# Split attention and a Fourier gate on one core: the expected flags' program in line with a late guard, sines of one token block rotated into the others, and a new written order

## The chip, the cores and the metric

The kernel runs on one core of a Trainium2 chip. The time is the device time of one execution in microseconds. A core has five engines that this kernel uses: TensorE (PE; its weight loads appear as PEld), VectorE (DVE), ScalarE (ACT), GpSimd (POOL) and SyncE (SP, which here issues most loads and stores). Each engine works through its own instructions strictly in their order and waits on semaphores for the others. The chip's DMA engines move data between HBM and the on-chip memory (SBUF); PSUM is the memory that matmuls write.

## What is computed

The attention takes q, k and v of shape 4 x 8 x 768 x 64. A flag for each of the 8 heads says whether it is a retrieval head (full causal attention) or not (4 sink columns and a window of 64). The inputs given mark heads 0, 2 and 6 as retrieval heads. Its output, 4 x 768 x 512, goes through a gate with a circular convolution over the 768 positions.

```python
scores = scale * np.matmul(q, k.transpose(0, 1, 3, 2))
causal = rel >= 0
stream_keep = causal & (is_sink | in_win)
mask = np.where(retr, full_mask, stream_mask)
scores = np.where(mask, scores, -1000000000.0)
a = np.exp(scores - np.max(scores, axis=-1, keepdims=True))
a = a / (np.sum(a, axis=-1, keepdims=True) + 1e-09)
attn_out = np.matmul(a, v)
...
proj = x @ w_proj
x1, x2, x3 = proj[..., :D], proj[..., D:2 * D], proj[..., 2 * D:]
X2 = np.fft.rfft(x2, n=S, axis=1)
H = np.fft.rfft(filter_fft, n=S, axis=0)[None, :, :]
y = x1 * np.fft.irfft(X2 * H, n=S, axis=1) * x3
return y @ w_out
```

## The kernel before

**Tiling.** The 32 (batch, head) items are worked on as 16 pairs of heads, four to a batch. Pair n belongs to batch n // 4 and to one of four kinds: RL, LL, RR or LL (R a retrieval head, L a local one), so that the blocks of scores that are computed at all are known when the program is built. The 768 tokens are six blocks of 128.

**Steps of a pair.** Loads of k, q and v (lk, lq, lv) on SP's queue; casts to bf16 (ck, cq, cv); six transposes each of k and q on PE (T, line 1447) and their copies out of PSUM (E, a copy of 128 x 768); score chunks on PE (sc, line 1492), to which a bias for masked positions is added by a matmul of the identity with the table btab (sb, line 1505) in the first four pairs, while later pairs mask after the exponential by a product (mk); the exponential on ScalarE (ex, line 1511); the product with v on PE (at, line 1556); the reciprocal of the row sums (rec, line 1562) and the normalised output f_attn (nm, line 1573) on VectorE. The columns kx and v_x are small copies that give the local heads their sink columns. Sums and differences of the two halves of a sequence (fe, fd, both f_fo) start the Fourier transform of the pair (W, line 1617; later pairs use thirds, uv and br).

**Steps of a batch.** Once its four pairs are done, the batch's spectrum X (line 1660), its products with the filter's spectrum HAB (pa, pb, pc on tiles P and m), the inverse transform c (line 1725), the three projections x1, x2, x3 (line 1695), the products that give gy (g, line 1714 and 1718, and y), and the output matmuls o (line 1758) with their evictions oe (f_o) and stores st. The filter's own spectrum F (line 1293) is made once, from the sums and differences of its two halves (fold, line 1285).

**The tables at the start.** The Fourier matrix G, 128 x 6 x 3 x 128 in bf16, is made of sines and cosines on the chip: integer angles (angle) and numbers of turns (turns) for three blocks of token positions, their difference (wrap, line 1201), its absolute value (size, line 1206), and four sine activations over all three blocks (sin1, sin2, cos1, cos2, line 1214). The causal and window masks are the seven 128 x 128 tables of mtab, cut out of ones on GpSimd (mtab1 in the opening; mtab2 and mtab3 at lines 1165 to 1183, behind the first casts); btab (line 1187) is made from mtab on VectorE.

**The two programs.** An opening runs first, which also compares the flags in memory with the expected ones (check). Every engine then loads the result into a register and branches (lines 1862 and 1863): with other flags a general program is run, written out in full in a sequence of its own (ORDER), else the patterned one.

**What sets the order.** The order of the patterned program is written out by hand in the text FAST: each word is an operation, @ names one of four PSUM slots (two banks each) and /v, /s, /p the engine where there is a choice. The opening's order is in OPENING. The operations are issued in that order on their engines, nothing is moved later. BLANKS gives the sizes of three groups of matmuls on a tile of zeros (blank0 to blank2, line 1143), 17 in all. The last block of 128 output rows is done in two halves (oe3.5 and oe3.6), which share one PSUM tile.

## Time and profile before

| what | us |
|---|---|
| three runs | 188.08, 188.29, 188.73 |
| median of the runs | 188.29 |
| span of the profiled execution, first to last instruction | 188.0 |
| TensorE busy | 171.7 |
| VectorE busy | 152.6 |
| ScalarE busy | 143.3 |
| GpSimd busy | 64.1 |

No time beside its span is given for the profiled execution, so the 0.3 us between span and median stand for what lies around it. In the rows below, a number such as L1447 is the line of the kernel. An arrow points from what is read to what is written; f_ is a prefix of the patterned program's tiles. A row of a timeline gives the start and the length of a run of like instructions and, in brackets, the idle time before it and what ended that. Busy times of TensorE are modelled from overlapping matmuls, so a busy TensorE isn't one at its peak.

### The profile page before, as it was taken

To read this page: it belongs to the slowest core of one execution; us is meant where nothing else is said; L and a number is where in the kernel's file an instruction comes from. 1 tells how busy PE (TensorE), PEld (TensorE's weight loads), DVE (VectorE), ACT (ScalarE), POOL (GpSimd) and SP (SyncE) were. 2 spreads that over 40 slices of the span, in tenths; PEclk is the share of its full clock that TensorE was granted. 3 is DMA by queue.
4 is the path that set the end of the run, shared out by engine and by line. 5 is a ranking of instruction groups with operands and counts; after the bars stand their busy time and mean duration, and the time that the engine had idled before them with its cause. 6 is when DMAs were issued, how large, how long until landed. Compare 5 with 4: busy or idle time off the path is not lost.

```text
span 188.0 us, 4376 instructions
## 1 busy us (share of the span) xinstructions
PE 171.7 (91%) x1688; PEld 103.9 (55%) x1704; DVE 152.6 (81%) x301; ACT 143.3 (76%) x191; POOL 64.1 (34%) x96
## 2 busy tenths in 40 slices
PE   0889996989999999999999999999999999999960
PEld 0346773644585556565556656475567644565430
DVE  6559676968999998998799999999799996388720
ACT  6689995879997998987999999899895526613330
POOL 3368750992080094443210111311406405400200
PEclk9999999999999999999999999999999999999998
DMA  5999999699999899999899988688942205300363
GB/s 182 309 271 281 194 187 287 151 260 228 218 210 203 180 192 210 184 232 234 193 249 257 225 180 176 137 138 225 127 125 55 112 2 157 122 3 0 113 248 104
DMA packets 77695, 33.67 MB, mean 179 GB/s; under 512 B 66850, under 2 KB 74082, under 8 KB 77666
## 3 DMA queue, kind: packets, MB, share of 16 engines
q1 hardware_dynamic: 74576, 30.29, 70.4%
q0 software_dynamic: 2944, 2.88, 10.1%
q8 instruction: 15, 0.25, 0.6%
q10 hardware_dynamic: 146, 0.13, 0.2%
q14 instruction: 14, 0.11, 0.2%
HBM read 24.64 MB, written 6.29 MB: 165 GB/s over the span
## 4 chain that ended last, share of the span: by engine, by line
PE 65%; DVE 14%; DMA 7%; POOL 4%; ACT 3%; issue 2%; SPq 0%; POOLq 0%; DVEq 0%
PE f_x_ps L1695 18%; PE f_X_ps L1660 10%; PE f_out_ps L1758 8%; PE f_c_ps L1725 7%; PE f_sc L1492 6%; PE f_att L1556 6%; DMA qk_ahead<-in_q_dram 4%; DMA f_qk_f<-in_q_dram 3%; DVE f_attn L1573 2%; ACT f_pT L1511 2%; PE f_W_ps L1617 2%; DVE f_P L1110 2%; PE f_sc L1505 2%; DVE f_fo L1110 1%; DVE turns L1736 1%
## 5 line engine op out<-in xcount | busy, mean ns | idle before, releaser
L1511 ACT ACTIVATE f_pT<-f_sc 128x1024 bf16<-128x1024 f32 (+3 forms) x68 | 58.7, 918 | 3.7 <-PE f_sc L1492 3.2
L1695 PE MATMUL f_x_ps<-f_xT,f_wproj 128*128 128x384 bf16 x256 | 46.7, 326 | 0.4 <-DVE f_attn L1573 0.3
L1695 PEld LDWEIGHTS <-f_wproj 128*128 128x128 bf16 x256 | 23.9, 98 | 16.5 <-issue 1.6
L1660 PE MATMUL f_X_ps<-f_wproj,f_xh 128*128 128x512 bf16 x92 | 22.3, 379 | 0.2
L1758 PE MATMUL f_out_ps<-f_wout,f_gy 128*128 128x512 bf16 x86 | 21.7, 379 | 0.3
L1492 PE MATMUL f_sc<-f_qkT 64*128 64x128 bf16 (+3 forms) x248 | 20.3, 250 | 0.0
L1725 PE MATMUL f_c_ps<-f_Gi,f_P 128*128 128x384 bf16 x96 | 18.4, 326 | 0.2 <-DVE f_gy L1714 0.2
L1110 POOL TENSOR_TENSOR f_fo<-f_attn 128x384 bf16<-128x384 bf16 x13 | 12.3, 954 | 15.0 <-DVE f_attn L1573 14.8
L1736 DVE TENSOR_TENSOR turns<-angle,f_c_ps 128x384 bf16<-128x384 f32 x32 | 16.3, 548 | 1.3 <-PE f_c_ps L1725 0.8
L1556 PE MATMUL f_att<-f_v_aug,f_pT 128*128 128x65 bf16 x392 | 17.2, 193 | 0.0
L1556 PEld LDWEIGHTS <-f_pT 128*128 128x128 bf16 x472 | 16.0, 97 | 2.1 <-issue 0.4
L1107 ACT COPY f_o<-f_out_ps 128x1024 f32<-128x1024 f32 (+2 forms) x12 | 10.2, 854 | 8.7 <-PE f_out_ps L1758 7.8
L1573 DVE TENSOR_TENSOR f_attn<-f_att,f_rec 128x768 bf16<-128x768 f32 x16 | 15.3, 955 | 0.6
L1492 PEld LDWEIGHTS <-f_qkT 64*128 64x128 bf16 x248 | 10.6, 94 | 9.3 <-issue 7.0
L1660 PEld LDWEIGHTS <-f_xh 128*128 128x128 bf16 x96 | 9.0, 98 | 10.3 <-issue 0.7
L1107 ACT CAST f_xh<-f_W_ps 128x768 bf16<-128x768 f32 x13 | 10.5, 807 | 4.5 <-PE f_W_ps L1617 2.3
L1758 PEld LDWEIGHTS <-f_gy 128*128 128x128 bf16 x92 | 8.6, 98 | 9.3 <-DVE f_gy L1718 0.3
L1107 ACT CAST f_X<-f_X_ps 128x1024 bf16<-128x1024 f32 x10 | 10.2, 1016 | 4.6 <-PE f_X_ps L1660 4.5
L1531 DVE TENSOR_TENSOR f_pT<-f_pT,mtab 128x1024 bf16<-128x1024 bf16 (+1 forms) x18 | 12.1, 688 | 1.4 <-ACT f_pT L1511 1.4
L1447 PE MATMUL f_qkT_ps<-identity,f_qk_bf 128*128 128x128 bf16 x96 | 7.9, 225 | 5.6 <-DVE f_qk_bf L1101 5.2
L1725 PEld LDWEIGHTS <-f_P 128*128 128x128 bf16 x96 | 9.0, 98 | 6.5 <-issue 0.6
L1110 POOL TENSOR_TENSOR f_br<-f_fo,f_uv 128x256 bf16<-128x256 bf16 x6 | 4.6, 765 | 21.3 <-DVE f_uv L1110 12.3
(132 smaller groups left out, 329.9 us busy)
## 6 DMA issues: line engine op xcount, KB each, us to landing
f_v_f<-in_v_dram SPq DMA_DIRECT2D x32, 192.0 KB, 4.4
out_dram<-f_o SPq DMA_DIRECT2D x17, 256.0 KB, 2.3
qk_ahead<-in_k_dram SPq DMA_DIRECT2D x6, 384.0 KB, 6.3
qk_ahead<-in_q_dram SPq DMA_DIRECT2D x6, 384.0 KB, 6.3
qk_ahead<-in_k_dram SPq DMA_DIRECT2D x10, 192.0 KB, 4.3
qk_ahead<-in_q_dram SPq DMA_DIRECT2D x10, 192.0 KB, 4.9
f_wproj<-in_moe_w_proj_dram POOLq DMA_DIRECT2D x6, 256.0 KB, 7.2
out_dram<-f_o SPq DMA_DIRECT2D x3, 512.0 KB, 4.4
```

Source lines behind the costliest of these rows:

```text
L1107: nc.scalar.copy(out=out, in_=in_)
L1110: (nc.gpsimd if now["engine"] == "p" else nc.vector).tensor_tensor(out, a, b, op)
L1492: nc.tensor.matmul(sc[:, bank, col:col + 128 * cnt], lhsT=keys, rhs=qkT(n)[rows, 0, 128 * i:128 * (i + cnt)], start=(col == 0 or not biase ...
L1511: nc.scalar.activation(out=pT(n)[:, c, :, 0:w], in_=held[f"sc.{n}.{c}"][:, :, 0:w], func=AF.Exp, scale=SCALE)
L1531: nc.vector.tensor_mul(some, some, near(c)[:, None].to_broadcast([128, 2, cols, 128]))
L1556: nc.tensor.matmul(att[:, hh, 65 * i:65 * i + 65], lhsT=pT(n)[:, c, bank, col:col + 128], rhs=values, start=(z == 0), stop=(z == len(here) ...
L1573: nc.vector.tensor_mul(attn(n).rearrange("p i hh d -> p hh i d"), rows[:, :, :, 0:64], held[f"rec.{n}"][:, :, :, None].to_broadcast([128, ...
L1660: nc.tensor.matmul(ps[:, u, :], lhsT=xh(b)[:, cc, chain, 128 * part:128 * part + 128], rhs=wproj()[:, cc, DM:2 * DM], start=(cc == 0), sto ...
L1695: nc.tensor.matmul(ps[:, s, 0:HS], lhsT=wproj()[:, cc, part * DM + cb * 128:part * DM + (cb + 1) * 128], rhs=xT(b)[:, cc, s * HS:s * HS + HS],
L1725: nc.tensor.matmul(ps[:, r, 0:HS], lhsT=P(b)[:, t, u, ch], rhs=Gi()[:, tile_no], start=(m == 0), stop=(m == 2))
L1736: fn(conv[:, half * HS:half * HS + HS], held[f"evs.{b}.{cb}"], held[f"c_ps.{b}.{cb}"][:, 1, 0:HS])
L1758: nc.tensor.matmul(ps[:, i % 2, :], lhsT=gy(b)[:, cb, i * 128:(i + 1) * 128], rhs=wout()[:, cb, :], start=(cb == 0), stop=(cb == NC - 1))
```

## The change

The branch at the start is gone. The opening and the patterned program run in line whatever the flags are. The comparison with the expected flags gives a number differ; near the end the guard looks at the reciprocals of all row sums, which now stay in one tile (recs): they have to lie between 2^-100 and 2^100 (gd0 to gd2; gd3 adds up 128 partitions by a 1 x 1 matmul; gd4 joins this with differ). All engines then load that value (flag), and behind the last store an If runs a general program, now made of loops, where it isn't zero. The bias constant of btab becomes 2^100.

The sines are made for one block of 128 positions alone (base, fp32) and rotated into the other two by a third of a turn: two scalings (gr) and four products (gm) on VectorE, one cast (gc) on GpSimd and three small ones (gs). Angles, turns, wrap and size shrink to a third. mtab2 joins the opening on GpSimd. Seven blank matmuls (warm) run in the opening; the 17 others are in eight groups. The two halves of the last output block get PSUM tiles of their own. The sequence FAST is new, and some operations change engines: of the 16 copies E, VectorE makes 10 instead of 4.

```diff
-BLANKS = (8, 3, 6)
+WARM = 7
+BLANKS = (2, 2, 2, 2, 3, 2, 2, 2)
...
-table sin0 tcol par fcol0 fcol1 ident mblank mtab0v quarter tfrac turns0 check angle0 mtab1 parb
+table mblank sin0 tcol par fcol0 fcol1 ident warm mtab0v quarter tfrac turns0 check angle0 mtab1 mtab2 parb
...
-angle1 turns1 angle2 ck1/p cq0/p turns2 lq2 ones0 ck0/v wrap1 T0.1@0 wrap2 blank0@1 wrap0 sin2 size E0.1/s sin1 lk2
+ck0/s mtab3 blank1@0 cq0/v wrap0 sin2 ones0 size T0.1@1 kz2 kz0 T0.0 ck1/p sin1 kz1 btab cq1/p E0.1/v E0.0/v lk3 cos1
...
-        nc.vector.tensor_scalar(out=btab(), in0=mtab(), scalar1=32768.0, scalar2=-32768.0, op0=ALU.mult, op1=ALU.add)
+        nc.vector.tensor_scalar(out=btab(), in0=mtab(), scalar1=FAR, scalar2=-FAR, op0=ALU.mult, op1=ALU.add)
...
-    trig("cos1", 0, 0, 256, lambda: G()[:, 0:4:3])
+    trig("cos1", 0, 0, 256, lambda: base()[:, 0:4:3])
...
+    @op("gc")
+    def _():
+        ev(G()[:, :, 0], base())
+    for i in range(2):
+        scaled(f"gr{i}", lambda i=i: turned()[:, :, i], lambda i=i: base()[:, 1 - i:5 - i:3], KAPPA if i == 0 else -KAPPA)
...
+                nc.vector.scalar_tensor_tensor(
+                    out=G()[:, tiles, m], in0=base()[:, tiles], scalar=0.5 if (u, m) == (0, 1) else -0.5,
+                    in1=turned()[:, u], op0=ALU.mult, op1=ALU.subtract if (u, m) == (1, 2) else ALU.add)
...
+    @op("flag")
+    def _():
+        pre["reg"] = nc.values_load(pre["other"][0:1, 0:1], min_val=0, max_val=1)
...
-    reg = nc.values_load(other[0:1, 0:1], min_val=0, max_val=1)
-    with tc.If(reg != 0, preferred_fallthrough_block=False) as cmp:
-        general(tc, ahead, pre, q, k, v, is_retrieval, n_sink, window, moe_w_proj, moe_filter_fft, moe_w_out, out)
-    with cmp.Else():
-        patterned(tc, ahead, pre, q, k, v, int(n_sink), int(window), moe_w_proj, moe_filter_fft, moe_w_out, out)
+    patterned(tc, ahead, pre, q, k, v, int(n_sink), int(window), moe_w_proj, moe_filter_fft, moe_w_out, out)
+    with tc.If(pre["reg"] != 0, preferred_fallthrough_block=False):
+        general(tc, local, q, k, v, int(n_sink), int(window), moe_w_proj, moe_filter_fft, moe_w_out, out)
```

How the order moves is shown at three places, as the instructions stand on an engine. The first is VectorE from the last part of the opening to the first copies of kT and qT (tfrac and the check's operations stand ahead of these rows); qk_ahead with 65 or 66 holds k and q of pair 0, f_qk_bf_2974 and f_qk_bf_135 their casts. Before:

```order
L1030 TENSOR_SCALAR angle<-fcol,tcol 128x384
L987 TENSOR_SCALAR par<-par 128x1
L1862 TENSOR_LOAD other
L1863 COMPARE_AND_BRANCH
L1196 TENSOR_SCALAR angle<-fcol,tcol 128x384 x2
L1101 CAST f_qk_bf_2974<-qk_ahead_65 128x768
L1201 SCALAR_TENSOR_TENSOR angle<-turns,angle 128x384 x3
L1206 TENSOR_SCALAR f_size<-angle 128x1152
L1101 COPY f_qkT_3005<-f_qkT_ps_2983 128x768
L1101 COPY f_qkT_3046<-f_qkT_ps_3039 128x768
L1187 TENSOR_SCALAR f_btab<-mtab 128x896
```

In the changed program, from the cast on, with tfrac and the check (want to differ):

```order
L546 CAST f_qk_bf_135<-qk_ahead_66 128x768
L417 TENSOR_SCALAR tfrac<-tcol 128x3
L1349 MEMSET want 1x8
L1352 MEMSET want 1x1 x3
L1353 TENSOR_SCALAR zeros<-flags 1x16
L1354 TENSOR_TENSOR local<-zeros 1x8
L1355 TENSOR_TENSOR differs<-local,want 1x8
L1356 TENSOR_REDUCE differ<-differs 1x1
L475 TENSOR_SCALAR angle<-fcol,tcol 128x384
L413 TENSOR_SCALAR par<-par 128x1
L670 SCALAR_TENSOR_TENSOR angle<-turns,angle 128x384
L675 TENSOR_SCALAR f_size<-angle 128x384
```

and directly behind them:

```order
L637 TENSOR_SCALAR f_btab<-mtab 128x896
L546 COPY f_qkT_175<-f_qkT_ps_150 128x768 x2
L682 TENSOR_SCALAR f_turned<-f_base 128x2x128
L546 COPY f_qkT_208<-f_qkT_ps_194 128x768
L682 TENSOR_SCALAR f_turned<-f_base 128x2x128
L546 COPY f_kx_170<-f_qkT_208 128x4x4
```

The cast (now of q0; k0's is on ScalarE) has moved ahead of tfrac and the check, the angle operations are one each, and btab stands ahead of both of pair 0's copies, which VectorE now makes in a row.

The second place is SP's queue of loads behind the four that the opening issues; qk_ahead with 65 or 66 takes pairs 0, 3 and 6 in turn, with 68 or 69 pairs 1, 4 and 7. Before:

```order
L1401 DMA f_qk_f_2_2977<-in_q_dram 128x2x384
L1401 DMA f_qk_f_2_2977<-in_k_dram 128x2x384
L1423 DMA f_v_f_1_3022<-in_v_dram 128x6x64 x2
L1401 DMA qk_ahead_65<-in_k_dram 128x2x384
L1423 DMA f_v_f_0_3026<-in_v_dram 128x6x64 x2
L1423 DMA f_v_f_2_3089<-in_v_dram 128x6x64 x2
L1401 DMA qk_ahead_65<-in_q_dram 128x2x384
L1401 DMA f_qk_f_5_3156<-in_q_dram 128x2x384
L1423 DMA f_v_f_3_3185<-in_v_dram 128x6x64 x2
L1401 DMA f_qk_f_5_3156<-in_k_dram 128x2x384
L1404 DMA f_qk_f_8_3302<-in_k_dram 128x6x64 x2
L1401 DMA qk_ahead_68<-in_k_dram 128x2x384
```

Now:

```order
L896 DMA qk_ahead_66<-in_k_dram 128x2x384
L896 DMA f_qk_f_2_182<-in_k_dram 128x2x384
L896 DMA f_qk_f_2_182<-in_q_dram 128x2x384
L918 DMA f_v_f_0_241<-in_v_dram 128x6x64 x2
L896 DMA qk_ahead_66<-in_q_dram 128x2x384
L918 DMA f_v_f_1_267<-in_v_dram 128x6x64 x2
L918 DMA f_v_f_2_313<-in_v_dram 128x6x64 x2
L918 DMA f_v_f_3_318<-in_v_dram 128x6x64 x2
L896 DMA f_qk_f_5_329<-in_q_dram 128x2x384
L896 DMA f_qk_f_5_329<-in_k_dram 128x2x384
L896 DMA qk_ahead_69<-in_k_dram 128x2x384
L896 DMA qk_ahead_69<-in_q_dram 128x2x384
```

The load of k3 has moved ahead of those of pair 2, v0 comes before v1, and k8 (f_qk_f_8) no longer stands between pair 5 and pair 4.

The third place is the end on ScalarE: the evictions f_o of the last output rows. Now:

```order
L552 COPY f_o_0_2926<-f_out_ps_0_2897 128x512
L552 COPY f_o_2_2934<-f_out_ps_4_2914 128x512
L552 COPY f_o_2_2934<-f_out_ps_5_0_2929 128x256
L666 TENSOR_LOAD other
L552 COPY f_o_1_2945<-f_out_ps_2_2938 128x512
L1273 DMA out_dram<-f_o_2_2934 128x256
L1363 COMPARE_AND_BRANCH
```

Before there were three evictions of 512 columns, then the second half eviction of 256, the store of 256 columns and a jump over the general program. One half eviction now stands ahead of the register load, the other is on VectorE, and the last eviction here is one of 512 columns.

More of the change, by code (lines that the diff above doesn't have):

```diff
@@ L16 @@
 SCALE = 0.125
+FAR = 2.0 ** 100
+LEAST = 2.0 ** -100
 CHUNKS = [
@@ L922, in _places, with opening @@
     return out
-def opening(nc, pool, pre, n_sink, window, check):
+def opening(nc, pool, psum, pre, n_sink, window, check):
     S = 768
@@ L1018, in _ @@
         )
+    @op("mtab2")
+    def _():
+        nc.gpsimd.affine_select(
+            out=mtab()[:, 1:6:2, :], in_=mtab()[:, 1:6:2, :], compare_op=ALU.is_ge, fill=0.0, base=window - 1,
+            pattern=[[0, 3], [-1, 128]], channel_multiplier=1,
+        )
+        if n_sink:
+            nc.gpsimd.memset(mtab()[0:n_sink, 1, :], 1.0)
+        nc.gpsimd.affine_select(
+            out=mtab()[:, 1:6:2, :], in_=mtab()[:, 1:6:2, :], compare_op=ALU.is_ge, fill=0.0, base=0,
+            pattern=[[0, 3], [1, 128]], channel_multiplier=-1,
+        )
+    @op("warm")
+    def _():
+        ps = psum.tile([128, 512], FP32, name="warm")
+        for _ in range(WARM):
+            nc.tensor.matmul(ps, lhsT=blank()[:, 0:128], rhs=blank(), start=True, stop=True)
     @op("exp0")
@@ L1161, in _ @@
         )
-    @op("mtab2")
+    @op("mtab2", "mtab2" not in OPENING.split())
     def _():
```

1030 lines of the change are left out of this document (293 added, 737 removed).

## The prediction

> **What bounds the kernel now.** The page comes first, for the engines' shares and the chain of work that ended last.
>
> ```profile
> PE 171.7 (91%) x1688; PEld 103.9 (55%) x1704; DVE 152.6 (81%) x301; ACT 143.3 (76%) x191; POOL 64.1 (34%) x96
> PE 65%; DVE 14%; DMA 7%; POOL 4%; ACT 3%; issue 2%; SPq 0%; POOLq 0%; DVEq 0%
> ```
>
> TensorE is busy for 91% of the span and carries 65% of the chain. The rest, 16.3 us of 188.0, has to be placed. The view by stretches gives, after the length, the busy time of PE, PEld, DVE, ACT and POOL, then granted clock, DMA share and GB/s:
>
> ```profile
> 5.00:10.00 5.00, 4.78 (x25) 2.27 (x26) 2.31 (x6) 3.47 (x6) 1.88 (x4) 1.00 0.99 318
> 10.00:15.00 5.00, 4.13 (x42) 2.29 (x40) 3.32 (x6) 4.27 (x6) 3.38 (x10) 1.00 1.25 254
> 15.00:20.00 5.00, 4.82 (x82) 3.33 (x81) 4.13 (x6) 5.00 (x7) 4.67 (x10) 1.00 1.09 283
> 20.00:25.00 5.00, 4.84 (x94) 3.83 (x92) 3.78 (x7) 4.64 (x7) 3.86 (x6) 1.00 0.98 179
> 60.00:80.00 20.00, 19.78 (x194) 11.88 (x192) 18.70 (x39) 18.99 (x28) 8.56 (x11) 1.00 1.13 195
> 80.00:100.00 20.00, 19.62 (x215) 11.75 (x215) 17.96 (x39) 18.17 (x24) 5.52 (x9) 1.00 1.04 234
> 100.00:120.00 20.00, 19.95 (x199) 12.77 (x198) 19.27 (x42) 18.60 (x26) 3.50 (x4) 1.00 0.93 183
> ```
>
> From 60 to 120 us PE is busy 59.35 of 60: there the matmuls themselves are the time, and the change keeps them. So a gain has to come from the first 45 us or from the tail. What PE does and waits for in the first part is in its timeline (start, length, instruction, idle before) and in the table of its waits (total, times, longest):
>
> ```profile
> 5.81 3.60 PE L1143 MATMUL f_blank_ps<-blank 128*128 128x512 bf16 x8
> 11.73 1.46 PE L1143 MATMUL f_blank_ps<-blank 128*128 128x512 bf16 x6
> 13.65 0.27 PE L1505 MATMUL f_sc<-f_btab,identity 128*128 128x128 bf16 x2 [0.46 <-DVE f_btab L1187]
> 45.09 2.76 PE L1660 MATMUL f_X_ps<-f_wproj,f_xh 128*128 128x512 bf16 x12
> PE f_qkT_ps L1447 <- DVE f_qk_bf L1101: 5.2, 1, 5.2
> PE f_F_ps L1293 <- DVE f_fold L1285: 1.4, 1, 1.4
> ```
>
> PE looks busy from 5 to 15 us, but 14 of its instructions there are blanks (5.06 us): idle time in disguise. PE starts at 5.2, the first biased score at 13.65. That one waits for btab; ScalarE's first exponential follows:
>
> ```profile
> 12.76 0.42 POOL mtab L1183
> 13.20 0.41 DVE f_btab L1187
> 12.75 1.28 ACT L1511 ACT_TABLE_LOAD   x1
> 14.04 8.79 ACT L1511 ACTIVATE f_pT<-f_sc 128x768 bf16<-128x768 f32 x11
> ```
>
> The first two are from the chain of waits: GpSimd's mask selects stand behind its casts, so mtab ends at 13.18 and btab at 13.61. From 14.04 the exponentials run without a pause (ACT 5.00 of 5 busy in 15 to 20); they set when the first four pairs are done. So **the start of that row is the number to move**.
>
> **The change, part by part.** *Start.* The selects move into the opening, ahead of the casts. But on VectorE the cast of q0 now stands ahead of tfrac, the check and angle. The rows for the steps, the second from the DMA issues of a narrow window (its last number: us from issue to landing):
>
> ```profile
> 1.33 0.45 SPq L1846 DMA_DIRECT2D qk_ahead<-in_q_dram x1
> qk_ahead<-in_q_dram SPq DMA_DIRECT2D x1, 384.0 KB, 3.7
> 13.51 0.56 DVE L1101 CAST f_qk_bf<-f_qk_f 128x768 bf16<-128x768 f32 x1
> 2.10 0.16 DVE L991 TENSOR_SCALAR tfrac<-tcol 128x3 f32<-128x3 f32 x1
> 3.37 0.13 DVE L987 TENSOR_SCALAR par<-par 128x1 int32<-128x1 int32 x1
> 5.01 1.49 DVE L1201 SCALAR_TENSOR_TENSOR angle<-turns,angle 128x384 f32<-128x384 int32 x3
> 6.53 0.76 DVE L1206 TENSOR_SCALAR f_size<-angle 128x1152 int32<-128x1152 int32 x1
> L1101 DVE COPY f_qkT<-f_qkT_ps 128x768 bf16<-128x768 bf16 x4 | 3.8, 957 | 3.6 <-PE f_qkT_ps L1447 3.6
> 6.53 0.52 ACT L1214 ACTIVATE f_G<-angle 128x384 bf16<-128x384 f32 x1 [1.63 <-DVE angle L1201]
> 9.61 0.93 ACT L1214 ACTIVATE f_G<-f_size,quarter 128x768 bf16<-128x768 f32 x1
> ```
>
> VectorE, step by step: q0 lands at 1.33 + 3.7 = 5.0; cast to 5.6; tfrac to par take 3.50 - 2.10 = 1.4, to 7.0; one wrap of three 0.5, to 7.5; size a third, 0.25; btab 0.41, to 8.2; the copies of kT and qT (E0.1, E0.0) 2 x 0.96, to 10.1. Score and bias on PE take some 0.7, so the first exponential can start at **10.8**. ScalarE is ready by then: its four sines are a third as long, between 0.3 and 0.5 each (estimate from 0.52 for 384 elements and 0.93 for 768), so from 7.5 they end near 9.1, and the table load at 10.4. Lead: 14.04 - 10.8 = 3.2. The ends: if one of the four kept 0.52 and three 0.93 (3.3 in all), the exponential would start at 7.5 + 3.3 + 1.28 = 12.1, a lead of 1.9; if the copies were no hindrance, ScalarE's 10.4 would hold, a lead of 3.6. I take 3.1, near the step-by-step value, since the elements are in fact a third.
>
> The skipped branch at the start is 0.4 us per engine, hidden behind the loads. The rotation that replaces two thirds of the sines is, on VectorE, two scalings and four products, at most 0.5 each by the wrap's row, some 2.5 us in all, and one cast of 0.83 on GpSimd. It lies beside exponentials; G is first needed for its transposes and W0, behind the first attention products; without that cover its 2.5 us would stand in VectorE's line ahead of the copies of pair 2. The seven warm blanks lie in the 5.2 us in which PE waits for loads. The larger bias constant and the guard's operations (four small ones on VectorE, one 1x1 matmul) cost under 1 us beside PE's last matmuls.
>
> *Up to X0 (45.09).* Fold waits for the filter, whose load is issued earlier, and F2 now stands behind more of the pairs' work: I take the wait of 1.4 as gone (ends: 0 and 1.4). k8 no longer stands ahead of k4 on SP. X0 thus starts 3.1 + 1.4 = **4.5** earlier, near 40.6.
>
> *After X0.* PE's matmuls are the same. Four blanks stand there (blank2, blank6), at 1.46 / 6 = 0.24 each: between 0 (in a wait) and 1.0; I take 0.5. Loads: the DMA engines are full from 5 to 100 us, so a lead may be paid back while pairs 4 to 15 are loaded. Ends: 0, and 2.7 (first rival); I take 1.0, nearer to 0 because PE waits for no load there.
>
> *Tail.*
>
> ```profile
> 181.64 0.42 DVE L1101 COPY f_o<-f_out_ps 128x256 f32<-128x256 f32 x1 [0.99 <-PE f_out_ps L1754]
> 182.10 0.37 ACT L1107 COPY f_o<-f_out_ps 128x256 f32<-128x256 f32 x1 [0.70 <-DVE f_o L1101]
> 182.57 0.38 SPq L1776 DMA_DIRECT2D out_dram<-f_o  x1
> q14 instruction: 6, 0.05, 2.5%
> out_dram<-f_o SPq DMA_DIRECT2D x1, 128.0 KB, 3.1
> ```
>
> The two half evictions follow one another now; with a PSUM tile each, ScalarE's 0.4 falls away. The flag's register load stands on every engine before its last work; at the start the same load and branch took about 0.6 us, hidden here if gd4 is done before the last matmul, else up to +0.6. From the last landing (182.57 + 3.1 = 185.7) to the end of the span are 2.3 us; I leave them, with ends of -2.3 and +2.3. The last two rows are those of the DMA view from 182.4 us on: instructions are fetched there. [...] No row shows what a single jump costs.
>
> Sum: 188.0 - 4.5 + 0.5 + 1.0 - 0.4 = 184.6 of span. The runs of before have a median of 188.29, 0.3 above the profiled span; kept, that makes **184.9**.
>
> **Rivals.** *Loads take the lead back.* For: DMA shares of 0.93 to 1.13 up to 120 us. Against: none of PE's listed waits beyond 0.5 us names a load directly. Only the hole at 20 to 25 us (179 GB/s after 283, SP waiting with k8) can then be filled: 5 x (1 - 179/283) = 1.8 us. 188.3 - 1.8 + 0.5 - 0.4 = **186.6**, a pay-back of 2.7.
>
> *The shorter jump at the end.* If the six instruction packets after 182.4 us hold up the end of the span and the looped block needs none of them, between 0 and 2.3 us go; with the half, 184.9 - 1.2 = **183.7**. Against: the stores land at 185.7 whatever is fetched, and what follows them has to be done in any case.
>
> *GpSimd slows VectorE (slower).* GpSimd gets three gy products more, four casts, one spectrum product, and four fo products less:
>
> ```profile
> L1110 POOL TENSOR_TENSOR f_gy<-turns,f_gy 128x768 bf16<-128x768 bf16 x1 | 1.8, 1757 | 7.0 <-DVE turns L1736 7.0
> L1110 POOL TENSOR_TENSOR f_m<-f_X,f_HAB 128x1024 bf16<-128x1024 bf16 x3 | 6.9, 2296 | 11.8 <-ACT f_X L1107 8.3 <-DVE f_P L1110 3.4
> L1110 POOL TENSOR_TENSOR f_fo<-f_attn 128x384 bf16<-128x384 bf16 x13 | 12.3, 954 | 15.0 <-DVE f_attn L1573 14.8
> 17.68 0.82 POOL L1103 CAST f_v_aug<-f_v_f 128x768 bf16<-128x768 f32 x1
> 17.70 0.87 DVE L1101 COPY f_kx<-f_qkT 64x256 bf16<-64x256 bf16 x1
> 82.47 0.22 DVE L1101 COPY f_kx<-f_qkT 64x256 bf16<-64x256 bf16 x1
> ```
>
> 5.3 + 3.3 + 2.3 - 3.8 = 7.1 us. The last three rows show the mechanism: a VectorE copy of 0.22 took 0.87 beside a GpSimd cast, 0.65 lost of 0.82. At that rate 7.1 us cost VectorE 5.6, with some 1.7 us of work moved to it (four fo, five v_x, less gy) 7.3. From 60 to 120 it has 60 - 55.93 = 4.1 free, part of it in waits that stay. With 2 us of it usable VectorE is 5.3 late: 184.9 + 5.3 = **190.2**; it turns slower when less than 3.3 is usable. Against: VectorE's share falls elsewhere, and much of GpSimd's work would have to meet a VectorE instruction that it slows. [...]
>
> *It doesn't start earlier.* The q0 cast ahead of the angles, or a late kT, holds the first exponential at 13 or later: lead under 1, and with the blanks **187.5 to 188.3**.
>
> **How the numbers follow.** Forecast with its own ends (183.8 to 186.2): 0.45. Shorter jump (182.3 to 184.4): 0.18. Loads: 0.15. GpSimd: 0.13. No earlier start: 0.09. This kernel's runs tell 0.3%, 0.56 us, from no change. Faster holds the forecast, the shorter jump, all of the loads' case and a little of the last: 0.45 + 0.18 + 0.15 + 0.01 = 0.79; same 0.07 of the last; slower 0.13 + 0.01 = 0.14. The low end, 182.3, is the forecast less the tail's 2.3 and a little; the high end, 188.3, takes in the loads' case and no earlier start and leaves GpSimd's case out.
>
> **What would show it.** Right: first exponential between 10.4 and 11.2, X0 between 40 and 42, PE busy as before from 60 on, both half evictions beginning within 0.3 us. Wrong: first exponential past 12 (the start), PE waits on casts or kT copies from 45 to 110 (loads), VectorE rows longer by tenths with GpSimd at work (contention), or over 3 us from the last landing to the end.

## The result, and the profile after

| | median us | lowest to highest, runs |
|---|---|---|
| before, on the same chip | 188.19 | 187.64 to 188.73, 4 |
| changed | 194.07 | 192.81 to 194.15, 4 |

The ratio is 1.0269, with a 95% interval of 1.0216 to 1.0322: the change makes the kernel slower by 5 us (the two medians lie 5.9 apart), where 184.9 had been forecast and 188.3 was the range's upper end. The profiled execution of the changed kernel took 194.07 us, with a span of 192.3. In this and all later runs the ratio leaves out executions that lie more than 1.5% above the fastest of their kernel; medians and ranges keep them.

The page of the changed kernel, its engines' shares and the engines of its chain:

```profile
PE 175.3 (91%) x1692; PEld 104.6 (54%) x1712; DVE 159.3 (83%) x315; ACT 137.1 (71%) x180; POOL 72.6 (38%) x103
PE 75%; DVE 14%; DMA 2%; ACT 2%; issue 1%; SPq 0%; DVEq 0%
```

TensorE still has 91%, now of a longer span, with 3.6 us more busy time; some matmul records are missing in both traces (before has 1688 on PE for 1704 weight loads, this one 1692 for 1712), so small differences of PE's busy time between these two mean little. The stretches (busy time of PE, PEld, DVE, ACT, POOL, then granted clock, DMA share, GB/s):

```profile
5.00:10.00 5.00, 3.23 (x27) 1.70 (x25) 4.58 (x17) 2.69 (x6) 2.82 (x5) 1.00 0.97 316
10.00:15.00 5.00, 4.25 (x30) 2.02 (x30) 4.29 (x9) 3.25 (x5) 3.26 (x6) 0.69 1.09 271
...
60.00:80.00 20.00, 19.17 (x189) 11.65 (x191) 18.84 (x37) 16.97 (x24) 6.64 (x8) 1.00 0.97 184
80.00:100.00 20.00, 19.68 (x226) 11.91 (x229) 17.82 (x40) 18.45 (x23) 6.95 (x10) 1.00 1.11 210
100.00:120.00 20.00, 19.90 (x181) 12.48 (x182) 18.82 (x39) 17.09 (x21) 9.05 (x10) 1.00 1.02 180
```

From 60 to 120 us PE is busy 58.75 of 60, against 59.35 before; in two traces with all records (e2 and e5 below) it is 59.86 and 59.57. The middle has not become the problem. Two other things have to be looked at, the start, where the clock was granted at 0.69 from 10 to 15 us, and the end.

**The end.** The timelines from the last matmuls on, and the last lines of the DMA view from 180 us on:

```profile
182.09 0.60 PE L1250 MATMUL f_out_ps<-f_wout,f_gy 128*128 128x256 bf16 x4
182.72 0.42 DVE L546 COPY f_o<-f_out_ps 128x256 f32<-128x256 f32 x1 [1.04 <-PE f_out_ps L1250]
183.06 0.40 SPq L1288 DMA_DIRECT2D out_dram<-f_o  x1
183.18 0.38 ACTq L1273 DMA_DIRECT2D out_dram<-f_o  x1
```

```profile
q14 instruction: 5, 0.04, 1.0%
q8 instruction: 1, 0.02, 0.5%
...
out_dram<-f_o SPq DMA_DIRECT2D x1, 128.0 KB, 2.5
out_dram<-f_o ACTq DMA_DIRECT2D x1, 128.0 KB, 4.4
```

The last matmul ends at 182.69 and the last store is issued by 183.56, but the span ends at 192.3. Before, the same rows stood at 181.61 and 182.95, and the span ended at 188.0. So of the 4.3 us by which the span grew, 1.1 had arisen by the last matmul, and 3.2 lie behind it, where from 183.2 on no engine computes. Against a second profile of before (e5 below, span 186.8) it is 5.5 us, 1.5 and 3.9. The trace's records of SyncE tell what stands there (start in us; what it is):

```
183.52  compare and branch, L1363 (the If)
183.62 to 185.12  four waits for stores to land
187.57 to 187.77  four more such waits
187.84  branch over the general program
190.62 to 191.32  twelve waits at the program's end, 0.06 apart
191.39 to 192.2   the engines' common end
```

SyncE stands still twice: 2.45 us within the waits that now come ahead of the jump (185.12 to 187.57), and 2.78 us behind the jump. The records of before hold one such stop behind the last store, 2.55 us (184.36 to 186.91), and a jump that took SyncE 0.51. There the jump and most of the stop lay beside the stores' flight: the last of them landed at 185.72. Here the last landed at 187.55, and the jump came after that; from there to the end it is 4.7 us, more than the 3 that the prediction had named as a sign of being wrong.

**The start.** The timeline of VectorE, ScalarE and TensorE:

```profile
7.62 0.86 DVE L675 TENSOR_SCALAR f_size<-angle 128x384 int32<-128x384 int32 x1
8.40 0.57 DVE L637 TENSOR_SCALAR f_btab<-mtab 128x896 bf16<-128x896 bf16 x1
8.90 1.80 DVE L546 COPY f_qkT<-f_qkT_ps 128x768 bf16<-128x768 bf16 x2
...
9.34 1.28 ACT L1006 ACT_TABLE_LOAD   x1
11.40 1.02 ACT L1006 ACTIVATE f_pT<-f_sc 128x1024 bf16<-128x1024 f32 x1 [0.78 <-PE f_sc L1000]
...
14.62 4.05 ACT L1006 ACTIVATE f_pT<-f_sc 128x1024 bf16<-128x1024 f32 x5 [0.91 <-PE f_sc L1000]
...
10.76 0.39 PE L987 MATMUL f_sc<-f_qkT 64*128 64x512 bf16 x2 [1.92 <-DVE f_qkT L546]
44.22 0.81 PE L1155 MATMUL f_X_ps<-f_wproj,f_xh 128*128 128x512 bf16 x3
53.84 0.81 PE L1155 MATMUL f_X_ps<-f_wproj,f_xh 128*128 128x512 bf16 x3
```

Before, the last piece of X0 was this:

```profile
51.17 0.81 PE L1660 MATMUL f_X_ps<-f_wproj,f_xh 128*128 128x512 bf16 x3
```

The first exponential starts at 11.40, 2.64 earlier than before. But the exponentials then pause, and X0, which ran from 45.09 to 51.98 before, begins 0.9 earlier (0.4 against e5), is broken into six pieces instead of four and ends at 54.65.

### The profile page after: what moved, and what is told of

Read it like the earlier page. It is cut to its first block, busy times and chain, and to the rows that moved or that the text cites. A ratio compares the mean times of both kernels' runs of the same rounds, so it can differ in the third digit from the quotient of the medians.

```text
span 192.3 us, 4398 instructions
## 1 busy us (share of the span) xinstructions
PE 175.3 (91%) x1692; PEld 104.6 (54%) x1712; DVE 159.3 (83%) x315; ACT 137.1 (71%) x180; POOL 72.6 (38%) x103
## 3 DMA queue, kind: packets, MB, share of 16 engines
q0 software_dynamic: 2944, 2.88, 10.0%
## 4 chain that ended last, share of the span: by engine, by line
PE 75%; DVE 14%; DMA 2%; ACT 2%; issue 1%; SPq 0%; DVEq 0%
PE f_x_ps L1190 21%; PE f_out_ps L1255 10%; PE f_X_ps L1155 9%; PE f_sc L987 8%; PE f_c_ps L1220 7%; PE f_att L1051 7%; PE f_sc L1000 2%; DVE f_HAB L682 2%; DVE f_pT L1026 2%; PE f_W_ps L1112 2%; DMA qk_ahead<-in_q_dram 2%; PE f_qkT_ps L942 2%; PE f_xt_ps L1124 2%; ACT f_pT L1006 2%; DVE turns L1231 1%
## 5 line engine op out<-in xcount | busy, mean ns | idle before, releaser
L987 PE MATMUL f_sc<-f_qkT 64*128 64x128 bf16 (+3 forms) x248 | 21.5, 257 | 2.7 <-DVE f_qkT L546 1.9
L1255 PE MATMUL f_out_ps<-f_wout,f_gy 128*128 128x512 bf16 x85 | 23.5, 380 | 0.3
L1051 PEld LDWEIGHTS <-f_pT 128*128 128x128 bf16 x472 | 17.4, 97 | 4.3 <-issue 0.6
L1051 PE MATMUL f_att<-f_v_aug,f_pT 128*128 128x65 bf16 x392 | 18.5, 193 | 0.5 <-DVE turns L1231 0.4
L555 POOL TENSOR_TENSOR f_gy<-turns,f_gy 128x768 bf16<-128x768 bf16 x4 | 6.6, 1642 | 25.3 <-DVE turns L1231 16.5
L1068 DVE TENSOR_TENSOR f_attn<-f_att,f_recs 128x768 bf16<-128x768 f32 x16 | 15.2, 951 | 0.3
L555 POOL TENSOR_TENSOR f_uv<-f_fo 128x256 bf16<-128x256 bf16 x10 | 7.1, 723 | 18.8 <-DVE f_fo L555 18.8
L555 POOL TENSOR_TENSOR f_fo<-f_attn 128x384 bf16<-128x384 bf16 x9 | 8.7, 971 | 14.3 <-DVE f_attn L1068 13.2
L548 POOL COPY f_kx<-f_qkT 128x16 bf16<-128x16 bf16 (+3 forms) x13 | 4.4, 345 | 22.9 <-ACT f_qkT L552 11.6
L552 ACT CAST f_x1s<-f_x_ps 128x768 bf16<-128x768 f32 x8 | 6.4, 805 | 8.7 <-PE f_x_ps L1190 8.7
```

What stands on the lines that cost most here:

```text
L552: nc.scalar.copy(out=out, in_=in_)
L555: (nc.gpsimd if now["engine"] == "p" else nc.vector).tensor_tensor(out, a, b, op)
L987: nc.tensor.matmul(sc[:, bank, col:col + 128 * cnt], lhsT=keys, rhs=qkT(n)[rows, 0, 128 * i:128 * (i + cnt)], start=(col == 0 or not biase ...
L1051: nc.tensor.matmul(att[:, hh, 65 * i:65 * i + 65], lhsT=pT(n)[:, c, bank, col:col + 128], rhs=values, start=(z == 0), stop=(z == len(here) ...
L1068: nc.vector.tensor_mul(attn(n).rearrange("p i hh d -> p hh i d"), rows[:, :, :, 0:64], recs()[:, n][:, :, :, None].to_broadcast([128, 2, N ...
L1255: nc.tensor.matmul(ps[:, i % 2, :], lhsT=gy(b)[:, cb, i * 128:(i + 1) * 128], rhs=wout()[:, cb, :], start=(cb == 0), stop=(cb == NC - 1))
```

## The experiments

Ratios are against runs of before on the same chip; the tail is the time from the end of the last matmul to the end of the span, in the profiled execution.

### The late If taken away, a low clock taken away, and both

e2 has neither the flag's register load nor the If and the general program; e1 puts eight blank matmuls into PE's idle time behind T1.1; e3 does both.

```diff
-o3.5.1@1 flag st3.4/v oe3.6/v st3.3/v
+o3.5.1@1 st3.4/v oe3.6/v st3.3/v
...
-    with tc.If(pre["reg"] != 0, preferred_fallthrough_block=False):
-        general(tc, local, q, k, v, int(n_sink), int(window), moe_w_proj, moe_filter_fft, moe_w_out, out)
```

```diff
-BLANKS = (2, 2, 2, 2, 3, 2, 2, 2)
+BLANKS = (2, 2, 2, 2, 3, 2, 2, 2, 8)
...
-T1.1@2 lq2 sc0.2@3
+T1.1@2 blank8@0 lq2 sc0.2@3
```

> The changed kernel with eight more blank matmuls between the transposes of k of pair 1 and the first score chunk, where TensorE was idle from 8.84 to 10.76 us and its granted clock then fell to 0.50 from 12 to 15 us. Theory (the clock loses the lead): the clock stays at 1.00 in 10 to 15 us, the exponentials run without the pauses of 0.9 and 0.8 us, and the span falls by 1.5 to 3 us. Rival (the new order loses it between 25 and 45 us whatever the clock): the clock is back, but the span falls by less than 0.7 us.

> The changed kernel without the register load of the flag and without the If with the general program; it computes the guard's value and leaves it unused, so other flags would give the patterned output. Theory (the late If puts the stores' landing, the branch and a fetch one behind the other): from the end of the last matmul to the end of the span it is 6.0 to 6.5 us instead of 9.6, the span falls by 3 to 3.6 us. Rival (the tail is set by the landing of the last stores alone, SyncE's waits would come in any case): less than 1 us.

> Both edits together: the eight blanks, and no flag load and no If (other flags would give the patterned output). If clock and late If are separate causes, the gains add up: span 192.3 less 4.5 to 6.5, that is 186 to 188. If the order is what lost the lead, it stays at 188.5 or more.

e1: 193.29 us (192.91 to 193.53), 1.0263 [1.0218, 1.0307]. e2: 188.62 (187.88 to 190.05), 1.0019 [0.9985, 1.0052]. e3: 188.44, 0.9991 [0.9948, 1.0034].

e2's timeline and the DMA view of its end:

```profile
182.09 0.60 PE L1246 MATMUL f_out_ps<-f_wout,f_gy 128*128 128x256 bf16 x4
182.94 0.33 SPq L1284 DMA_DIRECT2D out_dram<-f_o  x1
```

```profile
q1 hardware_dynamic: 864, 1.44, 29.7%
q10 hardware_dynamic: 144, 0.13, 2.9%
...
out_dram<-f_o SPq DMA_DIRECT2D x1, 128.0 KB, 2.0
out_dram<-f_o ACTq DMA_DIRECT2D x1, 128.0 KB, 2.2
```

This is the cleanest comparison of all. The last matmul ends at 182.69 in both kernels, and the span at 186.4 here and 192.3 there. No instruction packets move at the end, SyncE doesn't stop for more than 0.82 us, and the whole slowdown is gone: 194.07 - 188.62 = 5.45 us. These two medians come from two chips; e1 and e3, which differ by the same edit on one chip, are 193.29 - 188.44 = 4.85 apart.

e1 shows what the clock was worth. The stretch from 12 to 15 us, of the changed kernel and of e1:

```profile
12.00:15.00 3.00, 3.00 (x24) 1.50 (x21) 2.29 (x6) 2.03 (x4) 2.70 (x6) 0.50 1.01 263
```

```profile
12.00:15.00 3.00, 3.00 (x30) 1.52 (x28) 2.91 (x7) 2.91 (x4) 2.65 (x5) 1.00 1.14 275
```

Behind PE's 1.92 us of idle time (8.84 to 10.76) the granted clock is 0.50 for these 3 us; with the blanks in that place it is 1.00, ScalarE is busy 2.91 of 3 instead of 2.03, and PE does 30 matmuls instead of 24. The first exponential isn't earlier for it (12.00 in e1 and 12.25 in e3, 11.40 and 11.94 without the blanks); it is the pauses behind it that go. The end moves by 0.8 us at most (194.07 to 193.29, and 0.2 between e2 and e3). In all, the clock was granted at 0.50 for 3.4 us (11.89 to 15.30), and 0.8 of 194 us is 0.4%.

### The late If alone, on the kernel before

e5 is the kernel before once more, e6 adds to it the late flag load and, behind its last store, a second If with the looped general program (also used in the early If). e7 has the looped general program in the early If and nothing else.

```diff
-st3.3 o3.5.0@3 o3.5.1
+st3.3 o3.5.0@3 flag o3.5.1
...
         patterned(tc, ahead, pre, q, k, v, int(n_sink), int(window), moe_w_proj, moe_filter_fft, moe_w_out, out)
+        with tc.If(pre["reg"] != 0, preferred_fallthrough_block=False):
+            general2(tc, local, q, k, v, int(n_sink), int(window), moe_w_proj, moe_filter_fft, moe_w_out, out)
```

> The kernel before, unchanged, for its span beside its time and for a complete set of matmul records. If time and span differ by 1.7 us here as they do in every run of the changed kernel, the profiled execution of before (span 188.0) was one that took about 189.7, and the change cost 5.9 us and not 4.3 of span: a typical span of before is then 186.3 to 187. If time and span are 0.3 apart, the changed kernel has 1.4 us more outside its span.

> The kernel before with nothing changed but this: near the end every engine loads the flag again and a second If with the looped general program stands behind the last store (the first If stays, its general program is the looped one). Theory of the late If: slower by 4 to 5.5 us, SyncE's branch comes only when all stores have landed, and the span's end follows 2.5 to 3 us behind it. Rival (the changed kernel's tail came from its own last instructions and store order): less than 1.5 us.

> The kernel before with the looped general program in place of the written-out one, in the same If at the start. By the length of the jump: VectorE, ScalarE and TensorE no longer stop for 3 to 4 us behind their last instruction, but SyncE's own stop stays, and as SyncE sets the end the time changes by less than 0.7 us. If SyncE's stop goes too, the time falls by 1 to 1.5 us.

e5: 188.53 us. e6: 194.91 (193.65 to 196.3), 1.0335 [1.025, 1.042]. e7: 189.17, 1.0031 [0.9999, 1.0063]. So the late If and its flag load alone put on 5.7 to 6.4 us (against e7 and e5), with none of the new order; 1.0 to 1.5 of that lies ahead of the last matmul (182.12, against 181.14 in e5 and 180.63 in e7). SyncE has three stops in e6: 2.48 in the waits, 2.86 behind the jump, 2.05 at a register operation behind that. The table of SyncE's waits of e6 names the first as a wait of its own line, as that of the changed kernel did:

```profile
SPq L2046 <- SPq L2046: 2.5, 1, 2.5
```

e7 tells of the rival of the shorter jump. With the looped block, the stops of the other engines behind their branch at the end fell from 3.01 (VectorE) and 4.06 us (ScalarE) before to 0.56 and 0.44. But SyncE, which had 0.51 there, now had 2.99, and nothing was gained.

### The If back at the start

e4 is the changed kernel with If and Else back at the start, as before, and without the guard's late use (differ alone decides).

```diff
-    patterned(tc, ahead, pre, q, k, v, int(n_sink), int(window), moe_w_proj, moe_filter_fft, moe_w_out, out)
-    with tc.If(pre["reg"] != 0, preferred_fallthrough_block=False):
+    reg = nc.values_load(differ[0:1, 0:1], min_val=0, max_val=1)
+    with tc.If(reg != 0, preferred_fallthrough_block=False) as cmp:
         general(tc, local, q, k, v, int(n_sink), int(window), moe_w_proj, moe_filter_fft, moe_w_out, out)
+    with cmp.Else():
+        patterned(tc, ahead, pre, q, k, v, int(n_sink), int(window), moe_w_proj, moe_filter_fft, moe_w_out, out)
```

> The changed kernel with the branch put back at the start, on the flags alone: the looped general program in the If, the patterned one in the Else, no guard by the row sums at the end (its value is computed and unused). Theory of the late If: the tail is as short as before the change, 6.4 us after the last matmul, and the span falls by 3 to 3.5 us; on VectorE tfrac and the check are again ahead of the cast of q0, so the first exponential comes at 10.4 to 11.0 instead of 11.4. Rival (it is the looped program's place at the end and its fetch that cost, not the branch's time): the tail stays above 8.5 us.

189.77 us (188.37 to 192.67), 1.006 [1.0023, 1.0097]. The first exponential starts at 9.43, 4.6 us ahead of before, and yet the last matmul ends at 181.65, against 181.14 in e5:

```profile
9.43 1.02 ACT L1002 ACTIVATE f_pT<-f_sc 128x1024 bf16<-128x1024 f32 x1 [0.48 <-PE f_sc L996]
```

This kernel therefore shows the lead being lost without the late If and without the low clock (granted 1.00 from 5 to 50 us). The busy time of ScalarE on the line of the exponentials alone (each with its table load of 1.28), of the kernel before, and then of e4:

```profile
5.00:25.00 20.00, 11.19 (x14) 1.00 1.08 258
25.00:30.00 5.00, 3.68 (x4) 1.00 0.98 232
30.00:50.00 20.00, 8.62 (x10) 1.00 1.04 224
sum 45.00, ACT 23.50; mean ACT 7.83
```

```profile
5.00:25.00 20.00, 13.12 (x15) 1.00 1.01 258
25.00:30.00 5.00, 1.03 (x1) 1.00 1.13 292
30.00:50.00 20.00, 9.66 (x11) 1.00 1.19 225
sum 45.00, ACT 23.81; mean ACT 7.94
```

Up to 25 us, 1.9 us more of exponentials are done; five microseconds later the changed order is 0.7 behind, and by 50 us the two are level (23.81 and 23.50). The changed kernel goes the same way: 12.70 by 25 us, 13.35 by 30, 23.76 by 50. From 25.34 to 29.73 its ScalarE makes no exponential at all; it has six copies and casts there one behind the other, as FAST orders them. How much of the lead that pause costs was not tried.

A wait that is e4's own stands in its timeline of VectorE and GpSimd, and in its table of PE's waits:

```profile
18.57 2.23 DVE L546 COPY f_v_x<-f_v_aug 64x520 bf16<-64x520 bf16 x1
...
21.28 0.22 DVE L546 COPY f_v_x<-f_v_aug 64x520 bf16<-64x520 bf16 x1
...
17.99 1.04 POOL L763 DMA_DIRECT2D f_filt<-in_moe_filter_fft_dram  x1
19.04 0.84 POOL L548 CAST f_qk_bf<-qk_ahead 128x768 bf16<-128x768 f32 x1
19.80 0.84 POOL L548 CAST f_v_aug<-f_v_f 128x768 bf16<-128x768 f32 x1
```

```profile
PE f_xt_ps L1120 <- DVE f_attn L1064: 1.7, 1, 1.7
```

Of two copies of the same size, the first takes 2.23 us while GpSimd issues the filter's load and casts, the second 0.22 when GpSimd is done. PE then waits 1.7 us for the normalised output that stands behind the copy. In the changed kernel, where the opening runs later, the same two copies took 0.29 and 0.22, so this wait is no part of its loss.

### The filter's load moved

e8 moves the filter's load from its place ahead of ex0.5 to behind vs2, e9 to ahead of cv1, both in e4.

```diff
-cv0/v lfilt ex0.5
+cv0/v ex0.5
...
-tn0@0 te0/v ex2.2 vx2/s vs2/p T3.0
+tn0@0 te0/v ex2.2 vx2/s vs2/p lfilt T3.0
```

> The changed kernel with the branch at the start (as in the run with the If put back), and the filter's load, which keeps GpSimd busy for 1.04 us at 17.99, issued later, behind the small copies of pair 2. In the run before, a VectorE copy of v_x that takes 0.29 elsewhere took 2.23 from 18.57 on, while GpSimd was busy without a break to 20.7, and TensorE then waited 1.69 for f_attn. Theory (GpSimd holds VectorE up): the copy takes under 1.4, the wait falls under 1.0 and the last matmul ends 0.7 to 1.5 us earlier. Rival (the copy waits for v's load and not for GpSimd): the copy ends at the same time. Against a gain: the filter lands later, and TensorE may wait for fold.

> The changed kernel with the branch at the start, and the filter's load issued earlier instead of later: ahead of the cast of v1, where GpSimd stood idle from 16.1 to 17.2. If both readings hold (GpSimd held VectorE's copy of v_x; the late filter made TensorE wait 3.5 for fold), the copy ends by 19.5 instead of 20.8, no wait for fold over 0.5 comes, and the last matmul ends 1.0 to 2.0 us earlier than 181.65. If the lead is given back in another place again, the last matmul ends within 0.5 of 181.65.

e8: 191.87 us (190.33 to 193.28), 1.0113 [1.0037, 1.0189]. e9: 190.59 (188.63 to 192.97), 1.0116 [1.0057, 1.0175]. In both the copy falls to 0.80 us. In e8 the wait for it is gone, but the filter then comes late, as its timeline of VectorE (fold, which waits for the load) and its table of PE's waits show:

```profile
33.66 0.96 DVE L780 TENSOR_TENSOR f_fold<-f_filt 128x1536 bf16<-128x1536 bf16 x1 [3.42 <-DMA f_filt<-in_moe_filter_fft_dram]
PE f_F_ps L792 <- DVE f_xT L546: 3.5, 1, 3.5
```

In e9 the waits fall to 0.8 (copy) and 0.4 (F), and its profiled execution, 188.63 us, has its last matmul end at 180.44, 1.2 ahead of e4; it is the fastest of e9's runs, and its median is not better than e4's. So GpSimd's hold on the copy is real; 1.2 us at the last matmul in a single execution is all that it was seen to cost, and the medians show no gain.

### The jump in another place

e10 is e4 with the patterned program as the one that is jumped to at the start, so that none is left at the end; e11 is e10 with e9's place for the load and without three groups of blanks; e12 does to the kernel before, with the looped general program, what e10 does to e4.

```diff
-    with tc.If(reg != 0, preferred_fallthrough_block=False) as cmp:
+    with tc.If(reg != 0, preferred_fallthrough_block=True) as cmp:
```

> The changed kernel with the branch at the start, but laid out the other way round: the looped general program stands first and is jumped over at 3.7 us, and the patterned one runs on to the end of the program without a far jump. Theory (SyncE's jump costs 2.5 to 3 us of instruction fetch wherever it stands): from the last matmul to the end 3.5 to 4.2 us instead of 6.4, as in the run without any If, and SyncE's first load behind the branch is issued 1 to 2 us later (6.0 to 7.0 instead of 4.95); the time falls by 1 to 2.5 us. Rival (it is the waits at the end that cost, not the jump): the tail stays above 5.5.

> Both edits of the two runs beside this one, and without the six blank matmuls that stand after 28 us (blank0, blank2, blank6; 0.21 to 0.29 us each on a busy TensorE). If the three gains add up: 2 to 4.5 us under the kernel before, 184 to 186.5. If TensorE's clock needs those blanks, the granted clock falls under 0.98 and the gain is smaller.

> The kernel before with the looped general program, laid out first and jumped over at the start, so that no far jump stands at the end. If the jump is what costs at the end: from the last matmul to the end 3.5 to 4.2 us instead of 5.6 to 7.0, and the time falls by 1 to 2.5 us less what the later first loads cost (0 to 1.5 us).

e10: 189.16 us, 1.0006 [0.9966, 1.0045]. e11: 188.15 (186.63 to 190.32), 0.9978 [0.9944, 1.0012], the lowest median of all, and still not to be told from before. e12: 191.34 (190.97 to 192.66), 1.0179 [1.0128, 1.023]. The tails are 3.6 to 3.8 us, two or three less than with a jump at the end, and the opening pays for it. ScalarE's first exponential in e10 (9.43 in e4) and the table of PE's waits; and a row of VectorE in e12:

```profile
12.39 1.02 ACT L1002 ACTIVATE f_pT<-f_sc 128x1024 bf16<-128x1024 f32 x1 [3.04 <-PE f_sc L996]
PE f_sc L983 <- DVE f_qkT L546: 3.0, 1, 3.0
```

```profile
8.98 1.59 DVE L1376 SCALAR_TENSOR_TENSOR angle<-turns,angle 128x384 f32<-128x384 int32 x3 [3.40 <-issue]
```

In e12 VectorE stands for 3.40 us in the opening with nothing to wait for that the profile shows, and the first exponential comes at 18.64, 4.6 later than before.

### What in the late If costs

e13 cuts the body of the late If to one small DMA, e14 keeps the flag's load and drops the If. In e13 the branch went ahead of the last two stores and waited for none of them, so that jump and waits went away together; e15 has eight DMAs that write the output, one for each of the eight semaphores on which SyncE's DMAs land in the changed kernel (13 to 15 on each), so that the branch stays behind the stores and waits for all of them. The general program is left out of all three.

```diff
     with tc.If(pre["reg"] != 0, preferred_fallthrough_block=False):
-        general(tc, local, q, k, v, int(n_sink), int(window), moe_w_proj, moe_filter_fft, moe_w_out, out)
+        for b in range(8):
+            nc.sync.dma_start(
+                out=out[b // 2, b % 2 * 384:(b % 2 + 1) * 384],
+                in_=q[b // 2, b % 2 * 4:(b % 2 + 1) * 4].rearrange("h (s u) d -> (h s) (u d)", u=8))
```

> The changed kernel with the body of the late If cut down to one small DMA on SyncE (the general program is left out, so that other flags would get no answer); the flag's register load, the If and its waits for the stores stay. Theory (the price is the jump over the long block, in series behind the landing of the stores): SyncE's stop of 2.8 us behind its branch shrinks below 0.5, the stores' waits stay ahead of it; the time is 188.6 (without the If) + 0.7 for the waits and the branch, some 189.3, at most 191.5 if the last store lands as late as in the changed kernel (2.2 later). Rival (the If as such, its waits and its register load, costs the time, whatever it jumps over): the stop stays near 2.8 and the time at 193 to 194.

> The changed kernel with the flag's register load on all engines but no If behind it (the general program is left out). Theory: the load is hidden beside the last matmuls, so this is as without the load and the If, 188.6, within 0.5. Rival (the register load ahead of the last evictions is part of the price): 189.5 or more, with the last store issued later than 183.3 us.

> The changed kernel with the body of the late If cut down to eight DMAs on SyncE that write the output (the general program is left out, so that other flags would get a wrong answer). They use all eight of SyncE's queues and the output, so that the branch stands behind the last store and the way past the body waits for all stores, as in the changed kernel; only the jump is short. Theory (the far jumps are the price): both of SyncE's stops behind its last store, 2.45 and 2.78 us, go, no instruction packets move then, the last matmul's end to the end of the span is 3.7 us and up to 0.9 for the second set of waits, and the time some 189 to 190. Rival (the wait for the landing, in series with the branch, is the price): the stop of 2.45 us in the waits stays, with the last store landing 4 us after its issue, 6 us or more from the last matmul to the end, and a time of 191 or more.

e13: 189.02 us (188.07 to 190.57), 1.0017 [0.9977, 1.0056]. e14: 189.15 (187.98 to 190.85), 1.0012 [0.9985, 1.0039]. e15: 190.2 (189.21 to 191.17), 1.0086 [1.0048, 1.0123]. Of e15, the table of SyncE's waits and the DMA view from 182 us on:

```profile
SPq L1363 <- SPq L1363: 2.1, 3, 1.0
```

```profile
q14 instruction: 1, 0.01, 0.2%
...
out_dram<-f_o SPq DMA_DIRECT2D x1, 128.0 KB, 2.2
out_dram<-f_o ACTq DMA_DIRECT2D x1, 128.0 KB, 2.7
```

The flag's load is all but free (e14 against e2, 0.5 us with overlapping runs). A late If with all its waits but a near jump costs 190.2 - 188.62 = 1.6 us (1.3 by the ratios), at or above the upper end of the 0.4 to 1.4 expected: there the branch took SyncE 0.19 us instead of 2.78, and the wait for the last store 1.04 instead of 2.45. The far jump is worth the other 194.07 - 190.2 = 3.9 us.

All profiled executions together bear this out. The stops are those of SyncE behind its last store that are longer than 2 us:

| kernel | stops | tail, us |
|---|---|---|
| e2, e3, e10 to e12 (no jump at the end) | none | 3.6 to 3.8 |
| e14 (flag load alone), e13 (near jump) | none | 4.3, 4.2 |
| e5 (before again), before | none; 2.55 | 5.7; 6.4 |
| e15 (near jump behind the waits) | none | 5.8 |
| e4, e8, e9; e7 (jump at the end of the Else's side) | 2.88 to 2.90; 2.99 | 6.4 to 6.5; 7.0 |
| e1; changed (far jump behind the waits) | 2.30 + 2.56; 2.45 + 2.78 | 9.4; 9.6 |
| e6 | 2.48 + 2.86 + 2.05 | 11.2 |

## Why the prediction was wrong

Two steps failed, of nearly the same size. The forecast span was 184.6 us and the profiled one 192.3. Up to the last matmul the sum had -3.0 (from 181.6 to 178.6), and it ended at 182.7: 4.1 us missed. Behind it the sum had -0.4 (from 6.4 to 6.0), and it took 9.6: 3.6 missed. The last 1.5 is that the time lies 1.8 above the span, where the prediction took the 0.3 of the text ahead of it. The second step alone would have meant no gain; that the kernel became slower is the first.

**The first step is the tail.** "From the last landing ... to the end of the span are 2.3 us; I leave them", with ends of -2.3 and +2.3, and the flag's load as the only new cost. Of the jump over the general block at the end, the prediction asked only whether it is shorter now. It did not ask *when* the jump is taken. Before, SyncE and ScalarE jumped as soon as their own work was issued (183.00 and 182.93 us), while the last stores were on their way (landed by 185.72). Now the jump belongs to an If behind the last store; SyncE first waits for all stores, then jumps, then does the waits of the program's end once more. e6 puts this on the kernel before (+5.7 to +6.4), e2 takes it off (-5.45), and e15 shows that most of it comes with the far jump (3.9) and some with the doubled waits (1.6). The tail grew by less than that, 3.2 to 3.9, because before had a jump in its tail too: 5.7 and 6.4 us, against 3.6 to 3.8 with none. Instruction packets move at the end of the changed kernel (six from 180 us on) and none in e2, and behind the near target of e15 SyncE's stop is 0.19 us instead of 2.78; more than this was not shown of why a far jump takes so long. The prediction's rival of the shorter jump had the wrong sign: the shorter block did spare VectorE and ScalarE their stops (0.56 and 0.44 us in e7), but not SyncE (2.99), whose stop now stood alone in the way.

**The second is that X0 starts 4.5 earlier, and that all but 1.5 of this reaches the end.** The lead at the first exponential was 2.64 instead of 3.1. VectorE's step size was put at a third of 0.76, 0.25, and took 0.86, btab 0.57 instead of 0.41; the copies ended at 10.70, not 10.1. A cast of GpSimd stood beside size, and in e4, where GpSimd was idle at that point, size took 0.36 and btab 0.39 (GpSimd of the changed kernel, then VectorE of e4):

```profile
7.12 1.15 POOL L548 CAST f_qk_bf<-qk_ahead 128x768 bf16<-128x768 f32 x1 [1.84 <-DMA qk_ahead<-in_k_dram]
```

```profile
6.34 0.36 DVE L671 TENSOR_SCALAR f_size<-angle 128x384 int32<-128x384 int32 x1
```

The order of the steps was right, the mechanism too, and the wait of fold fell to 0.2 as forecast. But the start of one stage was taken as a measure of work done. The start of X0 moved by 0.9 and its end the other way, because the new order spreads its matmuls among other work. In e4 the first exponential even led by 4.6 us, and the last matmul came 0.5 later than before. In the row sums above, the lead in exponentials is used up by 30 us. What PE itself had done can be counted in the traces that hold all matmul records, without the blanks:

| matmuls begun by | before (e5, e7) | changed, without the late If (e2) | changed, early If (e4) |
|---|---|---|---|
| 50 us | 451, 460 | 450 | 461 |
| 120 us | 1190, 1192 | 1185 | 1190 |

An earlier exponential brings the end nearer only if PE has done more of its work by the point where it becomes the bound, and it had not. Where each tenth of it went is not settled: 0.2 to 0.8 to the clock (e1, e3), 0.7 in the opening to size and btab beside GpSimd's work, the rest to the order itself, which was not taken apart further.

**The smaller terms.** The half evictions did get tiles of their own, but begin at 181.42 and 182.72, not within 0.3 us of each other, since the order puts four other matmuls between their own. The 0.5 us for blanks was not measured by itself; e11 without three groups of them is within 0.3%. Without its late If the changed kernel is 1.5 us later at the last matmul than e5 and has a tail 2.0 shorter, which leaves the ratio of 1.0019: against the forecast of -3.0 up to the last matmul, that is 4.5 us missed.

**The rivals.** None of them held the late If. The one case that was slower, GpSimd's 190.2, would have had the right sign for another reason: GpSimd did slow VectorE, at places that the prediction had not priced (0.7 us in the opening here, a copy of 2.23 in e4), but not at the price of 5.3, since PE lost nothing between 60 and 120 us (59.86 in e2, 59.57 in e5). That loads take the lead back holds for the filter alone, and only where its load was moved (e8). The bounds of the tail, ±2.3, were set from a row that shows a landing, not from what would newly stand behind it.

## What to carry to other kernels

Of a branch at the end of a program, ask what it puts in series: what must have landed before it may be taken, and how far it jumps. Here it cost 5.45 us (the changed kernel against e2), 3.9 of them with the far jump (against e15). Beside the stores' flight a far jump was cheaper but not free: the tails were 5.7 to 7.0 us, against 3.6 to 3.8 with no jump at the end. An earlier start of a stage is a gain only if the bounding engine has more of its work done at the point where it becomes the bound; count that engine's useful work up to there, without blanks, not the start of one of its steps, in the old order and the new. In e4 the first exponential came 4.6 us earlier, 461 matmuls had begun by 50 us against 451 and 460, and the last one ended 0.5 later than in e5.

## What was not expected of the hardware

What a far jump took at the end differed from engine to engine and with the block that is jumped over. Over the block written out in full it was 0.51 us on SyncE, 3.01 on VectorE and 4.06 on ScalarE (before); over the looped one 2.6 to 3.0 on SyncE in every run, and 0.4 to 0.6 on the two others, except in e6, where they had 2.9. What decides this was not tried. Another stop of nearly the same length, 2.3 to 2.5 us, stands among SyncE's waits for stores in the changed kernel, e1 and e6, and it is of another kind: the store itself landed late. These traces record a store's landing in 16 parts. In the changed kernel 14 parts of ScalarE's last store had landed by 185.82 and the last at 187.55, and SyncE's wait ended at 187.57 (e1: 187.32 and 187.34; e6: 186.55 and 186.56). That is 3.3 to 4.4 us after such a store's issue, against 1.8 to 2.7 in every kernel without a far jump at the end. Instruction packets moved meanwhile (one of 16 KB from 184.76 to 185.71 in the changed kernel); that they held up the last parts fits, but was not tried. The 2.55 us of before are different again: the store that this wait names had landed at 184.89, and all stores by 185.72, yet the wait ended at 186.91. What SyncE stood for there stays open. Time and span are 1.7 to 1.8 us apart in every execution that gives both (188.53 and 186.8 in e5), not the 0.3 that the prediction took; the execution shown for before was thus probably one of about 189.7.
